# Seven matmuls that nobody reads, a last product taken bank by bank, and a new order for 3800 units

## The chip, the cores and the metric

The kernel runs on one core of one Trainium2 chip. The metric is device time in microseconds of one execution, inputs and outputs in device memory. Before the change the median of three runs is 907.4 us (907.23 to 908.23). Engines are named TensorE (PE in the rows; PEld is its loading of weights), VectorE (DVE), ScalarE (ACT), GpSimd (POOL) and SyncE (SP, which here only issues transfers).

## The reference

Attention over pooled keys and values, and a gated feed-forward layer on its result. All is float32.

```python
# q, k, v: (8, 8, 576, 64); w_gate, w_val: (512, 1536); w_out: (1536, 512)
k_p = k.reshape(B, H, 72, 8, D).mean(axis=3)
v_p = v.reshape(B, H, 72, 8, D).mean(axis=3)
scores = scale * np.matmul(q, k_p.transpose(0, 1, 3, 2))
scores = scores - np.max(scores, axis=-1, keepdims=True)
attn = np.exp(scores)
attn = attn / (np.sum(attn, axis=-1, keepdims=True) + 1e-09)
attn_out = np.matmul(attn, v_p)
x = np.ascontiguousarray(attn_out.transpose(0, 2, 1, 3)).reshape(4608, 512)
gate = 1.0 / (1.0 + np.exp(-(x @ w_gate)))
out = (gate * (x @ w_val) @ w_out).astype(np.float32)
```

## The kernel before

The 4608 tokens are cut into nine blocks of 512. The first block is done alone: its attention, its two products with the gate and value weights, and its product with the output weights. The other eight go in four pairs, where a scheme of seven block products in place of eight is used. Products of the feed-forward layer run on operands that are split into a high and a low part, three passes for each (`chain` is a bank of the first layer, `acc` one of the second).

The heads are taken two at a time, so a block has four pairs of heads. For each pair of the first block: VectorE adds up the keys in groups of eight (`keys`, the rows `early<-h`, later `early<-raw`), ScalarE places the sums on a block diagonal (`kbd`), TensorE makes the scores in two halves (`sc`), VectorE takes the maximum and subtracts it, ScalarE takes the exponential, VectorE sums and multiplies by the reciprocal (`main`, whose result is a 512-column tile), TensorE turns it (`tp`), ScalarE copies the turned tile out, and TensorE multiplies by the values (`av`). The 8 keys of 72 that don't fit into 64 rows go apart, as `rest`, `r` and `tr`. GpSimd clears the `kbd` tiles, places keys of later blocks, makes some low parts of the weights, and issues some transfers. A score instruction in float32 appears as two passes in the rows.

The order of all this is neither that of the code nor a scheduler's. Every instruction is taken down in a book, a few of them together as one unit (`Book.unit`), and the units are then issued in the order of a long table of numbers, `LATER`, one list for all engines; each engine runs its instructions in that order. So a unit waits behind those ahead of it in the list on its own engine, and for its operands. All instructions are issued from the helper `call` (line 317), so that all rows have that line.

The part that the change touches in the code is the last product (`second_sums`, line 1069, with `result`, line 1073) and the beginning of `first_pass` (line 1147). In `second_sums` each unit `(m, q)` multiplies a piece of the hidden layer with a piece of the weights, for two row blocks `k` and two banks `c`. The last results go out in half rows: ScalarE copies 256 columns out of the bank, SyncE sends them, and so on, four times.

Of the kernel before, what the change touches and what calls it, by code (L numbers as in the profile page):

```python
# [19 lines left out]
P = 128  # L20
# [9 lines left out]
BT = 512  # L30
# [82 lines left out]
5 4 3 6 0 10 2 7 24 13 17 19 20 8 26 12 27 18 16 30 9 22 21 75 25 34 36 35 46 32 1 44 39 54 38 40 11 29 47 28 51 15 31  # L113
65 52 66 37 61 57 41 67 62 42 14 60 63 53 73 82 45 74 70 87 79 71 97 136 84 123 77 112 109 111 80 88 100 99 101 96 98
59 83 104 91 105 89 81 106 72 130 78 107 110 93 92 95 94 58 114 127 115 116 119 125 86 103 120 128 197 144 122 143 142
135 141 85 137 138 129 157 205 140 147 145 121 102 204 134 132 153 154 152 133 155 151 131 222 90 108 139 118 161 203
164 149 124 162 148 216 126 163 156 167 150 166 189 170 158 169 174 159 165 146 171 190 160 55 168 177 179 243 172 173
117 178 56 193 180 186 230 181 223 182 199 244 233 201 196 206 200 202 209 185 184 33 188 225 192 49 191 176 195 240
175 236 183 187 234 226 247 239 238 250 245 251 259 217 248 257 282 253 242 258 212 279 283 64 276 252 232 261 286 267
237 43 269 211 278 50 256 274 219 268 254 218 277 266 265 231 275 272 241 280 221 299 288 298 284 228 305 227 229 285  # L120
289 292 113 302 290 281 293 255 235 273 294 303 316 300 246 326 332 329 304 333 335 301 311 287 318 331 330 328 327
317 334 307 308 306 198 309 314 352 322 260 312 315 325 362 324 353 208 364 291 345 323 366 339 313 346 348 338 365
349 321 340 296 399 350 360 310 215 376 68 342 405 361 341 297 358 343 214 344 69 367 347 295 263 382 355 373 370 337
264 374 380 224 375 270 271 377 336 371 386 387 356 385 354 395 357 372 398 396 397 393 411 392 403 402 48 207 368 391
400 412 363 417 406 410 407 369 419 378 404 409 401 388 418 416 389 408 414 413 424 426 320 447 319 425 23 423 381 427
422 262 379 446 429 420 384 434 421 383 194 444 430 220 457 437 435 431 578 466 436 483 441 485 443 452 449 451 492
210 428 469 470 467 468 464 461 493 462 213 463 450 432 433 497 486 500 390 440 487 415 501 448 438 456 584 471 484
472 480 498 481 477 490 439 458 473 517 482 502 249 478 479 460 521 513 465 474 491 475 499 530 454 453 531 590 488
532 527 476 510 522 489 524 528 394 525 445 523 685 529 504 526 507 495 540 546 496 516 545 505 459 519 506 514 494
455 511 534 442 544 533 542 512 503 577 541 551 548 520 582 535 556 518 549 557 558 76 596 567 560 568 570 571 536 569  # L130
611 564 543 603 574 572 550 580 606 581 351 565 515 555 566 561 554 612 562 539 573 604 576 607 632 563 605 597 600
579 598 552 583 608 538 601 537 602 599 648 622 623 559 642 629 553 627 669 359 678 636 575 628 672 953 659 656 675
588 591 679 613 585 633 586 676 667 660 593 595 594 589 680 666 587 592 673 614 677 609 670 610 621 508 674 615 630
618 624 626 697 634 700 509 689 616 631 635 617 619 637 690 620 643 625 639 649 682 684 671 694 701 653 652 640 686
645 646 687 650 651 698 699 655 702 657 691 703 692 662 638 647 641 695 654 696 681 711 708 658 668 663 644 714 693
661 726 704 715 665 547 706 727 664 707 709 710 712 683 717 718 729 720 722 713 719 725 724 705 721 730 731 728 737
735 723 952 743 760 733 761 747 745 954 736 746 739 738 752 748 740 755 762 744 768 732 765 763 955 751 758 759 775
756 757 764 767 782 766 805 750 753 771 993 806 754 772 1101 787 777 770 774 783 769 789 784 795 800 776 788 797 716
779 801 780 807 785 793 741 792 773 799 804 819 825 822 796 794 816 956 831 786 778 802 815 823 781 840 828 824 817
829 833 803 850 851 826 810 830 867 852 820 827 853 809 854 871 864 837 855 821 847 848 808 856 818 742 857 841 878  # L140
849 879 881 882 749 863 883 858 734 902 921 688 875 903 862 836 884 811 925 904 813 814 880 917 791 812 885 861 838
832 876 872 859 994 844 957 888 835 1056 843 996 845 889 842 865 886 920 866 868 891 899 958 890 905 870 992 860 1102
900 877 961 869 893 873 834 892 874 901 839 1103 1104 959 906 960 894 962 922 1106 895 915 995 978 908 923 972 1105
932 1048 979 1046 924 981 918 846 896 897 1047 887 973 909 941 898 907 933 911 938 942 982 1110 934 980 935 926 929
983 912 913 936 1111 1107 949 1112 790 1049 997 1108 919 1113 939 1109 998 1166 999 943 1050 1002 1051 910 1000 1001
937 969 1057 927 1134 1022 916 1063 940 944 914 1023 1093 950 946 963 945 964 1058 1027 947 951 965 1167 984 966 1024
# [1423 lines left out]
```

## Time and profile before

| | |
|---|---|
| median of 3 runs | 907.4 us |
| the profiled execution | 906.58 us |
| its span, first to last instruction | 904.8 us |
| TensorE busy | 891.4 us |
| VectorE busy | 657.4 us |
| ScalarE busy | 544.5 us |
| GpSimd busy | 200.0 us |

The profile is of one execution. The span is shorter than the time of the execution, which has a start and an end outside of the engines' instructions. A row of the view in order of time has the start, the length, the engine, the operation with its written and read tiles, a count where equal instructions follow each other, and in brackets how long the engine was idle before it and what ended that. Matmuls overlap: a pass is listed as 0.39 us although the next one starts 0.23 us after it, so that costs of passes are taken from the length of a run of them, not from one.

### The profile page before, as it was taken

How to read it: one execution, taken by the hardware profiler on the slowest of the kernel's cores; microseconds unless marked ns; L12 is line 12 of the kernel's file. 1: busy time of each engine (PE TensorE's matmuls, PEld its weight loads, DVE VectorE, ACT ScalarE, POOL GpSimd, SP SyncE). 2: the span in 40 equal slices, each digit the busy share in tenths (PEclk: the TensorE clock that was granted, in tenths of full speed). 3: DMA queues.
4: the chain of work that ended last, by engine and by line, in shares of the span. 5: the costliest groups of instructions: out<-in, count | busy, mean ns of one | idle time of the engine just before them, and what ended most of it. 6: DMA issues, size and time to landing. Idle time of an engine off the chain costs nothing.

```text
span 904.8 us, 12625 instructions
## 1 busy us (share of the span) xinstructions
PE 891.4 (99%) x4148; PEld 732.7 (81%) x4148; DVE 657.4 (73%) x1038; ACT 544.5 (60%) x1110; POOL 200.0 (22%) x369
## 2 busy tenths in 40 slices
PE   6999999999999999999999999999999999999998
PEld 5788878888888888888888888888888888888886
DVE  7989888889899999756668796355589552224863
ACT  5998998788978476545375555445365552224352
POOL 2422101012164235443443104132213000000000
PEclk9999999999999999999999999999999999999999
DMA  9899888889999888787987877676747776645554
GB/s 337 309 326 336 301 335 298 298 285 338 320 324 316 276 287 286 237 299 259 308 276 237 244 273 264 229 268 194 264 122 252 245 249 207 228 167 204 192 169 143
DMA packets 100433, 237.56 MB, mean 263 GB/s; under 512 B 13872, under 2 KB 34992, under 8 KB 98832
## 3 DMA queue, kind: packets, MB, share of 16 engines
q1 hardware_dynamic: 85328, 203.97, 66.6%
q0 software_dynamic: 15040, 32.79, 10.4%
q8 instruction: 33, 0.54, 0.2%
q14 instruction: 32, 0.26, 0.1%
HBM read 176.02 MB, written 60.69 MB: 262 GB/s over the span
## 4 chain that ended last, share of the span: by engine, by line
PE 81%; ACT 2%; DVE 1%; issue 0%; ACTq 0%
PE chain L317 50%; PE acc L317 25%; PE av L317 3%; PE sc L317 3%; ACT hs L317 0%; DVE s L317 0%; DVE hs L317 0%; PE tp L317 0%; DVE h L317 0%; ACT e L317 0%; ACT L317 0%; ACT raw_o L317 0%; DVE w_o L317 0%; ACT w_o L317 0%; ACT oparts L317 0%
## 5 line engine op out<-in xcount | busy, mean ns | idle before, releaser
L317 PE MATMUL chain<-xo,parts 128*128 128x512 f32 x2316 | 544.1, 392 | 0.5 <-ACT xs L317 0.5
L317 PEld LDWEIGHTS chain<-xo,parts 128*128 128x128 f32 x2316 | 430.7, 188 | 93.3 <-issue 1.0
L317 PE MATMUL acc<-hs,oparts 128*128 128x512 f32 x1008 | 237.0, 391 | 0.2 <-issue 0.2
L317 PEld LDWEIGHTS acc<-hs,oparts 128*128 128x128 f32 x1008 | 188.1, 188 | 40.6 <-DVE hs L317 1.2
L317 POOL DMA_DIRECT2D turned<-turn x240 | 131.7, 551 | 214.3 <-DVE turn L317 184.3
L317 DVE TENSOR_TENSOR y<-chain,sV 128x512 f32<-128x512 f32 x46 | 31.1, 686 | 69.6 <-PE chain L317 54.7
L317 ACT CAST hs<-h 128x1024 fp32r<-128x1024 f32 x52 | 54.3, 1051 | 27.2 <-PE acc L317 22.4
L317 DVE TENSOR_TENSOR hs<-h,hs 128x1024 fp32r<-128x1024 f32 x52 | 63.0, 1217 | 10.5 <-ACT hs L317 10.3
L317 ACT COPY chain<-chain 128x512 f32<-128x512 f32 x46 | 26.5, 577 | 52.8 <-PE chain L317 45.8
L317 DVE TENSOR_TENSOR y<-chain,sG 128x512 f32<-128x512 f32 x46 | 31.2, 682 | 34.2 <-PE chain L317 23.4
L317 ACT CAST hs<-s 128x1024 fp32r<-128x1024 f32 x36 | 37.5, 1050 | 28.5 <-DVE s L317 13.0
L317 DVE TENSOR_TENSOR hs<-s,hs 128x1024 fp32r<-128x1024 f32 x36 | 43.8, 1218 | 11.1 <-ACT hs L317 10.9
L317 ACT COPY sG<-chain 128x512 f32<-128x512 f32 x46 | 26.6, 584 | 41.0 <-PE chain L317 39.4
L317 ACT ACT_TABLE_LOAD x37 | 47.5, 1283 | 0.6
L317 ACT COPY sV<-chain 128x512 f32<-128x512 f32 x46 | 26.7, 584 | 34.0 <-PE chain L317 32.7
L317 ACT ACTIVATE gate<-chain 128x512 f32<-128x512 f32 x46 | 26.9, 594 | 31.8 <-PE chain L317 29.4
L317 DVE TENSOR_TENSOR h<-chain,gate 128x512 f32<-128x512 f32 x46 | 30.7, 679 | 20.1 <-PE chain L317 20.0
L317 PE MATMUL sc<-kbd,raw 128*128 128x144 f32 (+1 forms) x262 | 41.4, 297 | 0.3 <-ACT pr L317 0.2
L317 PEld LDWEIGHTS sc<-kbd,raw 128*128 128x128 f32 (+1 forms) x262 | 33.5, 176 | 8.6 <-issue 2.8
L317 ACT ACTIVATE gate<-y 128x512 f32<-128x512 f32 x46 | 28.9, 632 | 17.0 <-DVE y L317 16.8
L317 PE MATMUL acc<-oparts,hs 128*128 128x512 f32 x144 | 38.7, 402 | 0.0
L317 DVE TENSOR_REDUCE m<-sc 128x4 f32<-128x288 f32 x48 | 21.7, 452 | 17.5 <-PE sc L317 17.2
(210 smaller groups left out, 1099.9 us busy)
## 6 DMA issues: line engine op xcount, KB each, us to landing
oparts<-keptS SPq DMA_DIRECT2D x48, 512.0 KB, 4.7
oparts<-keptO SPq DMA_DIRECT2D x72, 256.0 KB, 4.7
raw<-in_wgv SPq DMA_DIRECT2D x12, 1024.0 KB, 8.1
out<-o SPq DMA_DIRECT2D x34, 256.0 KB, 3.8
raw<-in_kT SPq DMA_DIRECT2D x28, 288.0 KB, 5.0
raw<-in_qT SPq DMA_DIRECT2D x29, 256.0 KB, 4.9
raw<-in_vm SPq DMA_DIRECT2D x24, 256.0 KB, 5.5
raw_o<-in_wo SPq DMA_DIRECT2D x12, 512.0 KB, 8.5
```

The costliest lines, as they stand in the source:

```text
L317: return self._book.take(lambda: f(*args, **named))
```

## The change

Three edits. Ahead of the first scores, seven matmuls are issued that multiply the last cleared `kbd` tile with itself and write a bank of which nothing is read. In the last unit of the last product the two banks are taken one after the other, bank 0 with both row blocks and then bank 1, where before each row block went over both banks. And the last results go out otherwise: bank 0 whole, by ScalarE and one transfer of SyncE; bank 1 in halves, one copied by ScalarE and sent from ScalarE's queue, one copied by VectorE and sent by SyncE. Besides, the table `LATER` is another one throughout.

```diff
 LATER = """
-5 4 3 6 0 10 2 7 24 13 17 19 20 8 26 12 27 18 16 30 9 22 21 75 25 34 36 35 46 32 1 44 39 54 38 40 11 29 47 28 51 15 31
...
-            if last and side and add is None:
-                for k in (0, BT // 2):
-                    nc.scalar.copy(t[:, k:k + BT // 2], bank[:, k:k + BT // 2])
-                    nc.sync.dma_start(outT[r:r + P, a + k:a + k + BT // 2], t[:, k:k + BT // 2])
+            if last and side and add is None and c:
+                x, y = slice(0, BT // 2), slice(BT // 2, BT)
+                nc.scalar.copy(t[:, x], bank[:, x])
+                nc.vector.tensor_copy(t[:, y], bank[:, y])
+                nc.scalar.dma_start(outT[r:r + P, a:a + BT // 2], t[:, x])
+                nc.sync.dma_start(outT[r:r + P, a + BT // 2:a + BT], t[:, y])
                 return
...
-            for k in range(2):
+            final = last and i + 1 == len(units)
+            for n1 in range(2):
                 with book.unit():
-                    for c in range(2):
+                    for k, c in ((0, n1), (1, n1)) if final else ((n1, 0), (n1, 1)):
...
-                if i == 0 and k == 1:
+                if i == 0 and n1 == 1:
...
+        idle = ps.tile([P, HT, 2 * KEYS], F32, name="idle", tag="tp")
+        with book.unit():
+            for _ in range(7):
+                nc.tensor.matmul(idle[:, 0], lhsT=kbd[RING - 1][:, :P], rhs=kbd[RING - 1], start=True, stop=True)
+
```

What the new table does at three places follows, as the instructions stand on an engine; a line with - is of before, one with + of the changed kernel. First TensorE at the program's start (`kbd_89` to `kbd_92` are the four pairs' keys of the first block, `kbd_93` is the fifth tile of the ring):

```order
+L317 MATMUL idle<-kbd_93 128x144 x7
 L317 MATMUL sc<-kbd_89,h 128x144 x4
 L317 MATMUL sc<-kbd_90,h 128x144 x4
 L317 MATMUL sc<-kbd_91,h 128x144 x4
+L317 MATMUL sc<-kbd_92,early 128x144 x2
 L317 MATMUL vr<-xs_220 96x2x64 x4
-L317 MATMUL sc<-kbd_92,early 128x144 x4
+L317 MATMUL sc<-kbd_92,early 128x144 x2
```

The seven stand ahead of all scores, and one half of the fourth pair's scores goes ahead of a product with values. On SyncE, at the same place, keys (`in_kT`) and queries (`in_qT`) of the first block and the block of constants (`in_const`) are sent for:

```order
+L317 DMA h<-in_kT 128x576
+L317 DMA h<-in_qT 128x512
 L317 DMA h<-in_kT 128x576 x2
 L317 DMA h<-in_qT 128x512
 L317 DMA h<-in_kT 128x576
+L317 DMA early<-in_qT 128x512
 L317 DMA cst<-in_const 128x133
 L317 DMA h<-in_qT 128x512
-L317 DMA h<-in_kT 128x576
-L317 DMA h<-in_qT 128x512
-L317 DMA early<-in_qT 128x512
```

The first query is now second and not third, the constants eighth and not fifth, one query ninth. The second place is VectorE where the first block's third and fourth pair of heads get their probabilities. Before (the `128x512` rows are these two products, the reductions of `raw` are keys of the second block, `vres` low parts of values):

```order
L317 TENSOR_REDUCE early<-early 128x8 x2
L317 TENSOR_SCALAR early<-early 128x16
L317 TENSOR_TENSOR vres_104<-vr,vres_104 32x128
L317 RECIPROCAL early<-early 128x16
L317 TENSOR_TENSOR rest<-early 128x128
L317 TENSOR_TENSOR early<-early 128x512
L317 CAST r_261<-rest 128x4x32
L317 TENSOR_REDUCE early<-raw 128x72
L317 TENSOR_TENSOR early<-early 128x512
```

And in the changed kernel:

```order
L317 TENSOR_REDUCE early<-early 128x8 x2
L317 TENSOR_REDUCE early<-raw 128x72
L317 TENSOR_SCALAR early<-early 128x16
L317 RECIPROCAL early<-early 128x16
L317 TENSOR_TENSOR vres_105<-vr,vres_105 32x128
L317 TENSOR_TENSOR rest<-early 128x128
L317 TENSOR_TENSOR early<-early 128x512
L317 CAST r_262<-rest 128x4x32
L317 TENSOR_TENSOR early<-early 128x512
```

The reduction of the next block's keys has moved from behind the first of the two products to ahead of both. The third place is ScalarE at the program's end, with what each instruction waits for in brackets. Before:

```order
L317 CAST hs<-h 128x1024 [waits DVE_49,PE_49] x2
L317 COPY o<-acc 128x256 [waits DVE_49,PE_49]
L317 COPY o<-acc 128x256
L317 COPY o<-acc 128x256 [waits PE_49]
L317 COPY o<-acc 128x256
```

And in the changed kernel:

```order
L317 CAST hs<-h 128x1024 [waits PE_49,Activation_49]
L317 CAST hs<-h 128x1024 [waits DVE_49,PE_49] x2
L317 COPY o<-acc 128x512 [waits DVE_49,PE_49]
L317 COPY o<-acc 128x256 [waits DVE_49]
L317 DMA out<-o 128x256 [waits DMAHW3_49,Activation_49]
```

Four copies became two, and the second waits for VectorE, whose copy of the other half of that bank is its last instruction.

## Rows read from the trace of the kernel before

**Rows 1.** The page, busy time of each engine, and VectorE and TensorE in 40 slices of the span.

```profile
PE 891.4 (99%) x4148; PEld 732.7 (81%) x4148; DVE 657.4 (73%) x1038; ACT 544.5 (60%) x1110; POOL 200.0 (22%) x369
...
PE   6999999999999999999999999999999999999998
...
DVE  7989888889899999756668796355589552224863
```

**Rows 2.** The page, the chain of work that ended last, by engine.

```profile
PE 81%; ACT 2%; DVE 1%; issue 0%; ACTq 0%
```

**Rows 3.** The table by stretches: from and to, length, then busy time of each engine with its instructions, the granted clock of TensorE, the share of DMA time, GB/s.

```profile
0.00:5.51 5.51, 0.00 (x0) 0.03 (x1) 1.48 (x2) 2.24 (x5) 2.63 (x21) 1.00 0.65 198
5.51:9.84 4.33, 4.33 (x16) 3.85 (x16) 3.19 (x8) 1.00 (x5) 0.00 (x0) 1.00 1.07 377
9.84:12.40 2.56, 2.20 (x16) 1.93 (x16) 2.56 (x7) 1.60 (x4) 0.00 (x0) 1.00 0.98 330
12.40:20.66 8.26, 6.61 (x38) 5.16 (x37) 8.13 (x24) 6.36 (x16) 1.03 (x1) 1.00 1.04 390
20.66:27.52 6.86, 6.86 (x35) 4.38 (x35) 6.61 (x12) 5.33 (x10) 3.90 (x5) 1.00 0.99 404
27.52:900.73 873.21, 871.39 (x4047) 717.39 (x4045) 635.48 (x989) 527.34 (x1072) 192.40 (x343) 1.00 0.77 260
900.73:904.80 4.07, 0.00 (x0) 0.00 (x0) 0.00 (x0) 0.65 (x3) 0.00 (x0) 0.93 0.38 131
```

**Rows 4.** The view in order of time, TensorE in the head.

```profile
5.51 4.33 PE L317 MATMUL sc<-kbd,h 128*128 128x144 f32 x16 [5.51 <-DMA h<-in_qT]
10.02 1.22 PE L317 MATMUL sc<-kbd,h 128*128 128x144 f32 x8 [0.18 <-issue]
...
14.95 0.55 PE L317 MATMUL tp<-cst,early 128*128 128x128 f32 x3 [0.91 <-DVE early L317]
...
20.66 0.63 PE L317 MATMUL tp<-cst,early 128*128 128x128 f32 x4 [0.56 <-DVE r L317]
...
27.52 12.55 PE L317 MATMUL chain<-xo,parts 128*128 128x512 f32 x54
```

**Rows 5.** The same view, VectorE in the head.

```profile
3.72 1.48 DVE L317 TENSOR_REDUCE early<-h 128x72 f32<-128x576 f32 x2 [3.72 <-DMA h<-in_kT]
...
6.66 0.75 DVE L317 TENSOR_REDUCE early<-h 128x72 f32<-128x576 f32 x1 [1.46 <-DMA h<-in_kT]
...
19.83 0.68 DVE L317 TENSOR_TENSOR early<-early 128x512 f32<-128x512 f32 x1
20.43 0.22 DVE L317 CAST r<-rest 128x128 fp32r<-128x128 f32 x1
20.56 0.74 DVE L317 TENSOR_REDUCE early<-raw 128x72 f32<-128x576 f32 x1
21.23 0.68 DVE L317 TENSOR_TENSOR early<-early 128x512 f32<-128x512 f32 x1
```

**Rows 6.** The same view, GpSimd's clearing of the `kbd` tiles and ScalarE's placing of the first keys.

```profile
0.78 0.83 POOL L318 MEMSET kbd<- 128x144 f32 x5
...
4.57 0.53 ACT L317 ACTIVATE kbd<-early 64x72 f32<-64x72 f32 x2 [2.33 <-DVE early L317]
```

**Rows 7.** The same view, SyncE's issue of the last query, and two groups of the view of transfers (KB of each, median us from issue to landing).

```profile
4.50 0.43 SPq L317 DMA_DIRECT2D early<-in_qT  x1
...
early<-in_qT SPq DMA_DIRECT2D x1, 256.0 KB, 5.2
...
cst<-in_const SPq DMA_DIRECT2D x1, 66.5 KB, 4.2
```

**Rows 8.** The view of waits, TensorE from 27 us on: all that is listed (in total, times, longest).

```profile
PE tp L317 <- ACT y L317: 0.5, 1, 0.5
PE chain L317 <- ACT xs L317: 0.5, 1, 0.5
PE tr L317 <- ACT early L317: 0.2, 1, 0.2
PE sc L317 <- ACT pr L317: 0.2, 1, 0.2
PE acc L317 <- issue: 0.2, 1, 0.2
```

**Rows 9.** The chain that ended last in order of time (start, length, what, passes), two long runs of passes.

```profile
733.37 108.45 PE chain L317 x474
...
844.54 47.60 PE acc L317 x210
```

**Rows 10.** The end of the program: the view in order of time, the instructions on the tile `o` (duration in ns as least, median and most), and the last transfers' group.

```profile
900.09 1.33 ACT L317 COPY o<-acc 128x256 f32<-128x256 f32 x4 [6.86 <-PE acc L317]
900.48 1.79 SPq L317 DMA_DIRECT2D out<-o  x4
...
L317 SPq DMA_DIRECT2D out<-o x10: 332/341/426, 880.1 to 901.9; - x10
L317 ACT COPY o<-acc x6: 372/379/589, 879.5 to 901.0; 128x256 f32<-128x256 f32 x4, 128x512 f32<-128x512 f32 x2
L317 DVE TENSOR_TENSOR o<-acc,sG x2: 684/688/691, 883.5 to 891.5; 128x512 f32<-128x512 f32 x2
...
out<-o SPq DMA_DIRECT2D x4, 128.0 KB, 1.8
```

## What was predicted before the result

> **What bounds the kernel now.** I read the page's busy shares first [rows 1]: TensorE is busy 99% of the span, VectorE 73%, and the chain of work that ended last is 81% TensorE [rows 2]. Then the table by stretches [rows 3], which says where the missing per cent lies. From 27.52 to 900.73 us TensorE is busy 871.39 of 873.21 us: only 1.82 us of visible idle in the long middle. Everything else lost is at the ends: 5.51 us before the first matmul, 0.36 us until 12.40, 1.65 us from 12.40 to 20.66, and 4.07 us behind the last matmul. So the change can gain in three places: head, middle, tail.
>
> In the head the view of instructions in order of time [rows 4] shows two things. The first 16 score passes take 4.33 us, the next 8 only 1.22. Per pass that is 0.27 against 0.15 us, though the table gives a granted clock of 1.00 in every stretch [rows 3]; I read the first as the 1.2 GHz level and the second as 2.4 GHz. But VectorE [rows 5] waits until 6.66 us for its third block of keys, and from there it hardly stops: 2.56 of 2.56 us and 8.13 of 8.26 us busy in the two stretches up to 20.66 [rows 3]. TensorE's last long wait, 0.56 us, ends at 20.66 with VectorE's release (it stands in the row as VectorE's "r"), just behind the product that makes the third pair's probabilities (19.83 plus 0.68); from 20.66 to 27.52, where the first chain matmul stands, TensorE is busy throughout [rows 3, 4, 5]. VectorE paces the head; the scores do not.
>
> The trace's execution took 906.58 us for a span of 904.8, so 1.78 us lie around it; the median of the runs is 907.4, 0.8 above the profiled one. I sum changes of the span and add them to the median.
>
> **Unread matmuls.** Seven instructions, two passes each by the count of the scores (4 instructions make 8 passes), so 14 passes. At the slow price of 0.27 they take 3.8 us. Their operand is the last of the five blocks that GpSimd clears by 1.61 [rows 6], so they run from about 1.65 to 5.4. Queued behind them stand all scores. The first could start at about 5.15, because the first query is now the second transfer and the first keys are placed on ScalarE by 5.10 [rows 6]; the delay of up to 0.3 us falls into VectorE's wait for keys. If they raise the clock, 16 passes shrink from 4.33 to 16 times 0.15, 2.4 us: 1.9 us off TensorE. Bounds: 1.9 gained if scores were on the path, nothing if VectorE covers them. I take nothing: VectorE has no wait for a score in it after 6.66. If that cover went, the gain would be back up to 1.9.
>
> **Order of the head.** The keys that VectorE reduces third are still the fourth transfer; what is gone ahead of its landing is the constant block, 66.5 KB beside four blocks of 256 to 288 KB that need until 6.66 [rows 5, 7], some 0.2 us at their rate. So VectorE begins its unbroken run about 0.2 us earlier. Against that the key reduction of the next block, which stood behind the product of the third probabilities, now stands ahead of it (the order, in the part on the change): 0.67 us from its start to the next one's [rows 5]. It was hidden; now it is on the path, since the first transposition of that product and, queued behind it, the first attention product wait for it. From there to the first chain matmul the same 8 transpositions, 4 small ones, 4 attention products and 5 scores follow as before, 6.86 us of TensorE work [rows 3]. Sum: +0.67 less 0.2, taken as +0.4. Bounds: -0.3 (the waits between dependent small VectorE operations are filled by the reduction) to +1.0. Late next would be ScalarE's copies of the transposed probabilities, 0.59 each; they are made beside the attention products.
>
> **Order of the middle.** 3800 units are laid out anew. The work is the same; only waits can change. At most the 1.82 us of visible idle can go, of which the two longest single waits, both for ScalarE, are 0.5 each [rows 8]. Besides, there are pauses too short to count as idle: 474 chain passes took 108.45 us, 0.2288 each, 210 accumulating ones 47.60, 0.2267 [rows 9]; 2.1 ns over 474 passes is 1 us in 108, and as much everywhere would be 8 us. No row shows TensorE waiting for GpSimd long enough to be listed [rows 8], so room for late results of GpSimd removes nothing that this trace shows. Nor does the trace show the new order; bounds are -3.8 (all visible idle and a quarter of the short pauses) and +1.8 (as much idle again). I take -0.4, a quarter of the visible idle, nearest to losing one of the two 0.5 us waits.
>
> **The tail.** Before, the last twelve passes alternate between two banks; ScalarE makes four half copies from 900.09 in 1.33 us, and SyncE issues four transfers from 900.48 to 902.27, each landing 1.8 us later [rows 10]. So the last issue, at about 901.9, sets the end. Now bank 0 is ready three passes earlier, 0.68 us, and one transfer carries it. Bank 1 is ready as before, when the third half copy began, 900.76. Its halves are copied by VectorE, then ScalarE: the order gives ScalarE's copy a wait for VectorE. Two copies of about 0.4 (the ScalarE ones took 0.38 each; VectorE's nearest row is 0.69 for 512 columns; both [rows 10]) end at 901.6, and ScalarE issues its own transfer then. That is 0.3 before 901.9. Bounds: -0.6 (the first half's transfer is what counts) to +0.4 (a first transfer on ScalarE's queue is slower; no row has one). I take -0.3. Nothing is queued behind these waits. The rule that speaks against more: the Trainium skill's "PSUM — Partial Sum Buffer", in "PSUM bank collisions raise a hardware error", says that two engines must not touch one bank's quadrant at once, two reads included. By it the halves cannot be copied side by side, which would have made the gain 0.7; the wait in the order is in line with it, and no run here shows the collision.
>
> **Sum.** 0 + 0.4 - 0.4 - 0.3 = -0.3; 907.4 - 0.3 = 907.1 us. Less than 0.2%, 1.8 us, is about what a measurement of this kernel cannot tell from no change (its three runs lie 1.0 apart).
>
> **Rivals.** (a) The new order takes the middle's pauses away: all 1.82 of visible idle and two of the 8 us of short pauses, with the tail -4.1, with the head -3.7: 903.7 at the far end, 905.0 at two thirds of it. For it: pauses are spread all over [rows 9]. Against: the work stays, and no single wait is longer than 0.5 [rows 8], so many places have to improve at once. Chance 0.22. (b) The middle gets new waits: plan and chip part somewhere, and as much idle is added as was there, 1.8, plus the head's upper bound, 1.0, less the tail: 907.4 + 2.5 = 909.9. For it: every wait of TensorE that the trace lists there is for a result 0.2 to 0.5 us late [rows 8], so producers already stand close ahead of their readers. Chance 0.12. (c) The clock falls back, the slower side. With faster scores, TensorE is through the first two pairs by about 8 us (9.84 less 1.9 [rows 4]) and has nothing until the third pair's query is there; that is now the ninth transfer, and the old ninth, issued at 4.50, landed 5.2 later, at 9.7 [rows 7]. That is a wait of 1.7 us or more behind the raised clock, where the longest one in the head before was 0.91 [rows 4]. If it falls there, the 6.61 us of passes between 12.40 and 20.66 run at the slow level for half or all of that stretch: +3.3 to +6.6, of which the stretch's 1.65 us of idle absorbs half at best; about +3 is left: 910.1. It decides once passes behind that wait show 0.27 again. Against: 0.91 us did not lower it. Chance 0.06. The Trainium skill's "TensorE: Matmul & The Clock Gate", in "HAM oscillation — how this bites in real kernels", says that waits between bursts put the array back to half rate; the trace shows no fall behind its own short waits, so it doesn't test that. (d) The unread matmuls pay in full, because a faster score lets VectorE do more before its keys come: -1.9 with the rest as summed, 905.2. Against: VectorE's three first key reductions stand ahead of any score in the new order. Chance 0.05.
>
> **Chances and range.** The forecast, no measurable change, 0.55. Faster by over 0.2%: (a) and (d), 0.27. Slower: (b) and (c), 0.18. The likeliest case alone lies between 905.8 and 908.7. The range takes in two thirds of (a) and (d) below and most of (b) above: 904.9 to 909.3.
>
> **What would show it.** In the new profile: scores from about 5.3 us at 0.15 per pass in their greater part (the clock), VectorE without idle from about 6.5 to 20 all the same (no gain from it); the third pair's transpositions at about 21.0 and the first chain matmul at 27.7 to 28.1 (the head's +0.4); visible idle of TensorE of 1 to 2 us from there to its last pass; last transfer issued at about 1.3 us behind the last pass's start, from ScalarE. The forecast is wrong if the first chain matmul stands before 27.0, or if visible idle in the middle is above 3 us, or if passes turn slow again after 8 us.

## The result and the profile after

The changed kernel takes 914.1 us, median of three runs (913.06 to 914.25); the ratio to the kernel before is 1.0063, 95% interval 1.0048 to 1.0079. It is slower, and outside the predicted range. A second series of the same kernel, run beside the experiments, gave 912.05 (six runs, 910.49 to 913.77), ratio 1.0043 (1.0026 to 1.0059). The profiled execution took 914.1 us for a span of 912.3.

The page: busy share of TensorE, the granted clock in 40 slices, and the chain that ended last by engine.

```profile
PE 898.4 (98%) x4162; PEld 738.0 (81%) x4162; DVE 656.2 (72%) x1039; ACT 544.0 (60%) x1108; POOL 203.4 (22%) x369
...
PEclk8999999999999999999999999999999999999999
...
PE 79%; ACT 9%; DVE 5%; DMA 5%; issue 2%; SPq 0%; DVEq 0%; ACTq 0%
```

The busy shares are those of [rows 1] within a percentage point. The shares of the chain can't be set beside [rows 2]: the chain of before is followed back only to 131.43 us of its span, this one to the start. In two traces of the old order whose chain reaches the start (`unread_again` and `tail_only`, both below) ScalarE, VectorE and transfers have 10% and 12% of it, here 19%. The table by stretches, cut where the granted clock changes (from and to, length, busy time of TensorE, weight loads, VectorE, ScalarE and GpSimd, clock, share of DMA time, GB/s), answers to [rows 3]:

```profile
5.50:12.22 6.72, 3.19 (x22) 2.79 (x23) 5.75 (x13) 2.19 (x7) 0.00 (x0) 1.00 1.03 348
12.22:19.05 6.83, 6.83 (x27) 5.91 (x26) 5.33 (x16) 3.16 (x8) 1.33 (x1) 0.50 1.02 402
19.05:30.23 11.18, 10.72 (x58) 7.39 (x56) 10.96 (x23) 9.66 (x20) 4.72 (x6) 1.00 0.75 296
30.23:193.13 162.90, 159.45 (x776) 129.12 (x774) 140.47 (x240) 143.44 (x343) 28.52 (x39) 1.00 0.87 311
193.13:196.54 3.41, 3.41 (x11) 2.76 (x9) 2.07 (x5) 0.67 (x2) 0.00 (x0) 0.50 0.62 194
196.54:908.00 711.46, 710.65 (x3264) 586.66 (x3264) 490.46 (x746) 382.55 (x726) 166.21 (x303) 1.00 0.75 248
908.00:912.30 4.30, 0.39 (x2) 0.00 (x0) 0.42 (x1) 0.37 (x1) 0.00 (x0) 1.00 0.33 122
```

Twice the granted clock is 0.50, the 1.2 GHz level: for 6.83 us in the head and for 3.41 us from 193.13 on. Before, the only stretch below 1.00 lay behind the last matmul (0.93 in [rows 3]). The time before the clock's first rise counts as 1.00 in these tables, although its passes take 0.27 us, so a figure below 1.00 tells of falls alone. Cut at the first chain matmul and at the start of the last pass, the account of the two profiled executions is:

| | before | after | difference |
|---|---|---|---|
| start to the first chain matmul | 27.52 | 30.23 | +2.71 |
| from there to the last pass's start (the middle) | 872.82 | 877.77 | +4.95 |
| from there to the end | 4.46 | 4.29 | -0.17 |
| span | 904.8 | 912.3 | +7.5 |

TensorE's waits in the middle, the two longest in the view (total, times, longest), against [rows 8]:

```profile
PE tp L317 <- DVE pm L317: 1.8, 1, 1.8
PE chain L317 <- ACT parts L317: 0.5, 1, 0.5
```

The first of them stands directly ahead of the fall of the clock at 193.13. In the head TensorE's rows, in order of time, answer to [rows 4]:

```profile
1.66 3.73 PE L317 MATMUL idle<-kbd 128*128 128x144 f32 x14 [1.66 <-POOL kbd L318]
5.50 1.22 PE L317 MATMUL sc<-kbd,h 128*128 128x144 f32 x8
7.98 1.22 PE L317 MATMUL sc<-kbd,h 128*128 128x144 f32 x8 [1.26 <-DMA h<-in_qT]
11.47 1.59 PE L317 MATMUL sc<-kbd,h 128*128 128x144 f32 x8 [2.27 <-ACT kbd L317]
12.86 1.30 PE L317 MATMUL sc<-kbd,early 128*128 128x144 f32 x4
```

The unread passes take 0.27 us each, the first scores behind them 0.15: the clock has risen before the first score. Then TensorE waits 1.26 us for the second pair's query and 2.27 us for ScalarE's placing of the third pair's keys, and four passes that take 0.73 us without a fall (`no_unread`, below) take 1.30. The second trace of the changed kernel waited only 0.43 us for the query, but again 2.27 us for the keys, and its clock was at half for 10.24 us:

```profile
11.58 2.29 PE L317 MATMUL sc<-kbd,h 128*128 128x144 f32 x8 [2.27 <-ACT kbd L317]
```

```profile
10.83:21.07 10.24, 9.49 (x34) 8.39 (x35) 8.26 (x23) 5.60 (x11) 1.50 (x1) 0.50 1.01 388
```

### The profile page after: what moved, and what is told of

The parts are those of the page before. It is cut to its first block, busy times and chain, and to the rows that moved or that the text cites. A ratio compares the mean times of both kernels' runs of the same rounds, so it can differ in the third digit from the quotient of the medians.

```text
span 912.3 us, 12659 instructions
## 1 busy us (share of the span) xinstructions
PE 898.4 (98%) x4162; PEld 738.0 (81%) x4162; DVE 656.2 (72%) x1039; ACT 544.0 (60%) x1108; POOL 203.4 (22%) x369
## 4 chain that ended last, share of the span: by engine, by line
PE 79%; ACT 9%; DVE 5%; DMA 5%; issue 2%; SPq 0%; DVEq 0%; ACTq 0%
PE chain L317 43%; PE acc L317 28%; PE sc L317 3%; PE av L317 3%; DMA raw<-in_qT 1%; ACT parts L317 1%; ACT e L317 1%; ACT L317 1%; DMA raw<-in_kT 1%; DMA raw<-in_wgv 1%; ACT raw L317 1%; DMA w<-keptWO 1%; DVE early L317 1%; DVE h L317 1%; ACT w L317 1%
```

## The experiments

The first chain matmul and the middle of every trace that is used below, with the median time (and its lowest and highest). The kernel before, run beside each series, had medians of 907.05 to 907.42 us:

| kernel | first chain | middle | time |
|---|---|---|---|
| before | 27.52 | 872.82 | 907.4 |
| after | 30.23 | 877.77 | 914.1 (913.06 to 914.25) |
| after, again | 31.53 | 876.17 | 912.05 (910.49 to 913.77) |
| no_unread | 28.18 | 875.00 | 912.47 (909.31 to 914.97) |
| unread_only | 27.80 | 872.94 | 906.45 (905.49 to 907.98) |
| unread_again | 27.55 | 872.80 | 906.85 (905.78 to 908.96) |
| bridge | 28.25 | 875.27 | 911.05 (908.53 to 914.33) |
| head_new | 28.79 | 872.53 | 908.85 (907.75 to 910.53) |
| mid_new | 27.16 | 875.43 | 909.9 (908.55 to 912.09) |
| key_after_pm | 30.53 | 874.39 | 910.79 (909.22 to 917.16) |
| key_no_unread | 30.13 | 874.81 | 910.89 (909.13 to 912.42) |
| early_new | 27.56 | 880.19 | 909.7 (908.35 to 914.35) |
| late_new | 27.83 | 874.28 | 909.06 (906.25 to 913.37) |
| late_turn | 27.99 | 874.56 | 908.89 (907.58 to 911.08) |
| mended_again | 28.37 | 874.50 | 909.1 (908.29 to 910.32) |
| tail_only | 27.90 | 873.12 | 907.33 (906.84 to 908.62) |

A trace is one execution, and the new order scatters: a row's trace need not lie at its median. In the eight traces with the old order in the head the first chain matmul comes between 27.16 and 27.99 us; in the five traces with the old order in the middle that takes 872.53 to 873.12.

**The unread matmuls, out of the new order and into the old one.** `no_unread`:

```diff
         with book.unit():
-            for _ in range(7):
-                nc.tensor.matmul(idle[:, 0], lhsT=kbd[RING - 1][:, :P], rhs=kbd[RING - 1], start=True, stop=True)
+            pass
```

> The changed kernel without its seven unread matmuls (the unit stays in the order, empty; order and tail as changed). Theory of the clock: the unread matmuls bring full speed at 5.4 us, the scores then run ahead of their data, TensorE waits 1.26 and 2.27 us, and the granted clock falls to half from 12.22 to 19.05 us; without them full speed comes only near 10 us and stays, the first chain matmul starts at 27.6 to 28.2 us instead of 30.23, and the time is 914.1 less 2.0 to 2.6, 911.5 to 912.1. Rival, that the new head order (key reduction ahead of the product) makes the loss: the first chain matmul stays at 29.5 us or later and the time at 913.5 to 914.3. Both expect the pause of 1.8 us near 191 us to stay.

The first chain matmul came at 28.18, as the theory of the clock has it, and the mean granted clock was 0.999 or 1.000 in all six executions (0.994 to 0.996 in the first three of the changed kernel). But the trace is of the fastest of the six, 909.31, and the median, 912.47, lies where neither put it, with a scatter of 5.7 us and no fall of the clock. It is no lower than the 912.05 of the changed kernel's second series. The pause at 191 us, which both expected to stay, wasn't in this trace. So the head was told right for this trace and the middle not understood: the kernel loses without any fall of the clock, and differently from execution to execution.

`unread_only` puts the same seven matmuls ahead of the old order:

```diff
+        idle = ps.tile([P, HT, 2 * KEYS], F32, name="idle", tag="tp")
+        with book.unit():
+            for _ in range(7):
+                nc.tensor.matmul(idle[:, 0], lhsT=kbd[RING - 1][:, :P], rhs=kbd[RING - 1], start=True, stop=True)
```

> The kernel before with nothing but the seven unread matmuls ahead of its first scores (old order, old tail). Theory of the clock: full speed from 5.4 us, a wait of 2 us or more for the third pair's operands, the granted clock back at half near 12 us; first chain matmul at 29.5 to 30.3 us instead of 27.52, time 909.4 to 910.2. Rival, that the order makes the loss: the first chain matmul within 0.3 us of 27.5 and 907.2 to 907.7. Middle and tail as before in both.

No loss: 906.45, ratio 0.9991 (0.9982 to 1.0001), and no fall of the clock in ten executions (0.999 or 1.000). The theory's expectation fell: unread matmuls alone don't bring the clock down. In this trace the clock rose only at 10.86, so it left open what an early rise does. Run again:

> The kernel before with the seven unread matmuls alone, a second time, since 906.45 against 907.26 was at the edge of what can be told. Theory that they help a little where the old order keeps the third pair's scores close behind the second's: 906.3 to 906.9 and no fall of the granted clock even where it rises before 7 us; rival, that it was chance: 907.2 to 907.6. Third, that an early rise of the clock is followed by a fall here too: single runs at 909 or above with a mean clock of 0.998 or less.

906.85, ratio 0.9994 (0.9984 to 1.0005): a gain is not told apart from chance. In this trace the clock rose at 6.32 and stayed. TensorE's first rows:

```profile
1.67 3.73 PE L312 MATMUL idle<-kbd 128*128 128x144 f32 x14 [1.67 <-POOL kbd L313]
5.58 1.57 PE L312 MATMUL sc<-kbd,h 128*128 128x144 f32 x8 [0.18 <-DMA h<-in_qT]
7.61 1.22 PE L312 MATMUL sc<-kbd,h 128*128 128x144 f32 x8 [0.45 <-DMA h<-in_qT]
10.00 1.25 PE L312 MATMUL sc<-kbd,h 128*128 128x144 f32 x8 [1.18 <-ACT kbd L312]
```

The waits are 0.45 and 1.18 us where the new order has 1.26 and 2.27: there ScalarE ends the third pair's placing at 11.42, behind an exponential, here at 9.94. One of twelve executions had a mean clock of 0.996, at 908.96, the highest, which all but meets the third of the sentences expected. A mean clock of 0.998 or less is what one slow stretch of 3.41 us makes of it. Counted over the executions of all runs with a change in the order or with unread matmuls, it was found thus:

| head | unread matmuls | executions with a fall |
|---|---|---|
| new order | seven | 25 of 29 |
| new order | none | 1 of 16 |
| new order | seven, and eleven in the waits (`bridge`, next, and the two kernels built on it) | 4 of 31 |
| old order | seven | 1 of 22 |
| old order, the new one behind it (`mid_new`, `early_new`, `late_new`, `late_turn`, below) | none | 3 of 42 |

So the fall comes as a rule where both meet, the unread matmuls and the new order's late third pair, and now and then with one of them or none. The mean doesn't tell where in an execution a fall lies.

**Work through the waits.** `bridge` leaves the new order as it is and adds unread matmuls ahead of the second and the third pair's scores:

```diff
+BRIDGE = {(0, 1, 1): 4, (0, 2, 0): 7}
...
         with book.unit():
+            for _ in range(unread):
+                nc.tensor.matmul(sc[:, 0], lhsT=kbd[RING - 1][:, :P], rhs=kbd[RING - 1], start=True, stop=True)
             for i in range(HT):
```

> The changed kernel with eleven more unread matmuls: four ahead of the second pair's scores and seven ahead of the third pair's, so that TensorE works through the waits of 1.26 and 2.27 us. Theory of the clock: where it has risen before 7 us it doesn't fall back, the first chain matmul starts at 28.0 to 28.5 us instead of 30.2 and the time falls by about 2. Where it rises only at 9 to 11 us, as in another kernel with unread matmuls, the eleven run at half speed, 0.27 a pass for 22 passes, and the third pair comes up to 2 us late. Rival, that the fall at 12 us doesn't hang on the waits: it comes as before, first chain matmul at 30 us or later, and the time is 914 or more.

```profile
5.31 1.22 PE L318 MATMUL sc<-kbd,h 128*128 128x144 f32 x8
6.37 1.14 PE L318 MATMUL sc<-kbd 128*128 128x144 f32 x8
7.63 1.22 PE L318 MATMUL sc<-kbd,h 128*128 128x144 f32 x8
8.68 1.88 PE L318 MATMUL sc<-kbd 128*128 128x144 f32 x14
10.98 1.25 PE L318 MATMUL sc<-kbd,h 128*128 128x144 f32 x8 [0.42 <-ACT kbd L318]
12.34 0.76 PE L318 MATMUL sc<-kbd,early 128*128 128x144 f32 x4
```

The rows `sc<-kbd` without `h` are the added ones. With TensorE at work the clock stays (granted clock 1.00 from 4.88 until behind the last matmul), and the first chain matmul comes at 28.25 instead of 30.23. Seven of the ten executions had a mean clock of 0.999 or 1.000; three, at 911.24, 912.53 and 914.33, had 0.998, and where their fall lay isn't known. The theory of the clock holds for the head: the fall hangs on the waits, and the first chain matmul is 2.0 us later with it. In the time of the whole kernel this can't be told from chance: against the 912.05 of the same series the median fell by 1.0, half of the 2 expected, within the scatter.

**Head and middle by themselves.** The tables were put together from both orders (`new` and `old`, in the numbers of the changed code):

```diff
-LATER = new
+LATER = new[:161] + [u for u in old if u not in new[:161]]
```

> The changed kernel with the old order behind the first chain matmul: the head stands in the new order with its unread matmuls, the 3,600 units behind it in the order of before, the tail as changed. Theory that the two losses add, each from its own stretch: first chain matmul near 30.2 us where the clock falls back (28.2 where it doesn't), the middle 872.8 to 873.3 us as before, time 907.3 + 2.7 = 910.0 where the clock falls, 908.0 where not. Rival, that a late head is made up later: 907.2 to 907.8.

908.85, 1.4 us over its kernel before, ratio 1.0010 (1.0000 to 1.0020): what the new head costs by itself, its order and its clock together. The middle is 872.53, no worse than before, and the clock was at half for 3.41 us in the head, from 11.45; eight of the ten executions had a fall. The theory's condition "where the clock falls" has degrees: with the new head the slow stretch was 3.41, 6.83 and 10.24 us in different traces, and the first chain matmul came at 28.79, 30.23 (30.53 in another) and 31.53. `mid_new` is the complement, without unread matmuls:

```diff
-LATER = new
+LATER = old[:156] + [u for u in new if u not in old[:156]]
```

> The changed kernel with the old order ahead of the first chain matmul and without the unread matmuls: old head, new order behind it, tail as changed. Theory that the new order loses by itself in the middle: first chain matmul at 27.5 to 28.0 us, the middle 875.0 to 877.8 us instead of 872.8 (both seen with this order), time 909.5 to 912.3, and more scatter than the kernel before, which lies within 1.5 us of its median. Rival, that the middle's pauses follow from the late head: 907.2 to 907.8.

909.9, ratio 1.0024 (1.0011 to 1.0037), middle 875.43, no fall in any of the ten executions: as the theory said. The new order loses 2.5 us in the middle by itself, with the old head and a full clock. The 1.4 of `head_new` and these 2.5 make 3.9 of the 4.6 that the second series of the changed kernel lost. That second series:

> The changed kernel as it is, a second time, beside the others of this call. Both theories expect 913 to 914.5; the pause at 191 us and the clock's fall behind it are expected again if the key's transfer is late in every execution, and are gone if that was chance (the kernel without unread matmuls showed no such pause in its one trace): then the middle is 874.5 to 875.5 us instead of 877.8.

The time, 912.05, is below the 913 that both expected at least. The pause at 191 us was 0.5 us this time, with no fall of the clock behind it, and another of 2.16 us stood at 464 us, where the first trace had none. So neither sentence on the pause was right: pauses come and go at several places.

**One pause, repaired.** In the changed kernel's first trace the rows around 191 us are (SyncE's issue, VectorE, TensorE):

```profile
181.06 0.83 SPq L317 DMA_DIRECT2D raw<-in_kT  x1
...
190.64 0.75 DVE L317 TENSOR_REDUCE ks<-raw 128x72 f32<-128x576 f32 x1 [2.01 <-DMA raw<-in_kT]
191.31 0.68 DVE L317 TENSOR_TENSOR h<-h 128x512 f32<-128x512 f32 x1
191.91 0.69 DVE L317 TENSOR_TENSOR pm<-e,rz 128x512 f32<-128x512 f32 x1
...
190.14 0.80 PE L317 MATMUL sc<-kbd,raw 128*128 128x144 f32 x6
192.74 0.73 PE L317 MATMUL tp<-cst,pm 128*128 128x128 f32 x4 [1.79 <-DVE pm L317]
```

VectorE stands still for a key block's transfer, 9.6 us after its issue; the product `pm` that TensorE needs next is two places behind. SyncE issued that transfer behind four others from 178.61 on. In the old order it stood behind one store and a query and landed after 3.6 us; in all seven traces with the old order there it took 3.4 to 5.1, in eight other traces with the new order there 6.7 to 10.2. That the place in SyncE's queue is the reason is likely and not shown by itself. `key_after_pm` moves one unit, number 1184:

```diff
-1184 1065 1046 1022 1264 1015 1260 1053
+1065 1046 1022 1264 1015 1260 1053 1184
```

> The changed kernel with one VectorE unit moved: the key reduction that waits 2.0 us for its transfer at 188.6 us is issued behind the product pm instead of two places ahead of it. Theory: that reduction is what holds pm back, so TensorE's pause of 1.8 us at 190.9 us goes, and with it the fall of the granted clock from 193.13 to 196.54 us: 1.96 us of pause and 1.75 us of slow passes less, 914.1 - 3.7 = 910.4 (910.0 to 911.0). Rival, that the reduction is needed as early as it comes (the copy to kbd and the scores behind it wait instead): the pause moves to a score some 2 us later and the time stays within 1 us of 914.1.

```profile
188.50 0.69 DVE L312 TENSOR_TENSOR h<-h 128x512 f32<-128x512 f32 x1 [0.70 <-DMA h<-keptwG]
189.11 0.68 DVE L312 TENSOR_TENSOR pm<-e,rz 128x512 f32<-128x512 f32 x1
190.45 0.75 DVE L312 TENSOR_REDUCE ks<-raw 128x72 f32<-128x576 f32 x1 [0.66 <-DMA raw<-in_kT]
...
190.07 0.66 PE L312 MATMUL tp<-cst,pm 128*128 128x128 f32 x4
```

The transfer is as late as before (10.2 us), VectorE still waits for it, and TensorE doesn't: no pause, no fall of the clock behind it (the head has its fall as before), the middle 874.39, 3.4 less than in the changed kernel's first trace, and the median 910.79 as expected. Beside the second series, whose trace had only 0.5 us of this pause, it is 1.3 less. The edit does what it was to do at its place; how often the pause came without it isn't known. With this edit and without the unread matmuls:

> The changed kernel without its unread matmuls and with the key reduction behind pm, both at once. Theory that the two causes are separate and add: against the 912.05 of the changed kernel beside the same runs, some 2 us for the head (first chain matmul at 28.2 instead of 30.2 to 31.5) and some 1.3 for the reduction (912.05 to 910.79), 908.8; range 908.3 to 910. Rival, that without the clock's fall the key's transfer is in time anyway, so that the second edit gives nothing more: as without unread matmuls alone, 911 to 912.5.

910.89: 2 us above what adding would give. In this trace the clock rose only at 15.88 and the first chain matmul came at 30.13; without unread matmuls the head can be late too. (Its first 24 score passes take 2.26 us for eight, the price at 1.2 GHz; in the seven other traces without unread matmuls the clock rose between 8.84 and 11.27.) The middle was 874.81. The rival's figure is the one that was met, but not for its reason; the run doesn't decide between them. Beside the 910.79 with the unread matmuls, taking them out gave nothing, as in `no_unread`.

**Where in the middle.** `early_new` takes the new order up to about 231 us and the old one behind it, `late_new` the reverse, both with the old head and no unread matmuls (`mid` is the table of `mid_new`):

```diff
-LATER = mid
+LATER = mid[:1298] + [u for u in old if u not in mid[:1298]]
```

```diff
-LATER = new
+LATER = old[:1298] + [u for u in new if u not in old[:1298]]
```

> Old head without unread matmuls, then the new order for the units up to about 231 us, then the old order; tail as changed. With the new order all the way behind the old head the time was 909.9 (907.4 before). Theory that the new order loses where transfers are dense, up to some 230 us (by 50 us from the first chain matmul its pauses stood 0.5, 1.2, 0.1 and 0.4 us above those of before, and 0.4 us above in all that follows): 909.5, 909.0 to 910.0. Rival, that the loss is spread evenly: a quarter of it, 908.0.

> The complement: the order of before up to about 231 us, the new order from there on; tail as changed, no unread matmuls. Theory that the loss lies ahead of 231 us: 907.4 + 0.4 = 907.8, 907.3 to 908.3. Rival, evenly spread: three quarters of the 2.5 us, 909.3.

909.7 (ratio 1.0032, 1.0019 to 1.0046) and 909.06 (1.0015, 0.9997 to 1.0032). The first is the theory's figure, the second is not: the two halves lose 2.65 and 2.0 against their kernel before, and the whole 2.5. Each half seems to suffice, though the interval of `late_new` just takes in no loss (its trace's middle, 874.28, is 1.2 us above the highest with the old order); the seam between two orders may have a price of its own, which these runs don't separate. But the trace of `early_new` is its slowest execution, 914.35, and shows the mechanism at a third place:

```profile
110.47 1.13 ACT L312 ACTIVATE w<-raw 128x1024 f32<-128x1024 f32 x1 [2.45 <-DMA raw<-in_wgv]
111.51 1.21 ACT L312 ACTIVATE raw<-raw,cst 128x1024 uint32<-128x1024 uint16 x1
112.62 0.57 ACT L312 CAST pr<-tr 96x512 fp32r<-96x512 f32 x1
...
113.24 0.76 PE L312 MATMUL sc<-kbd,raw 128*128 128x144 f32 x4 [1.74 <-ACT pr L312]
```

ScalarE waits 2.45 us for a weight block, the copy `pr` stands behind it, TensorE waits 1.74 us, and from 115.52 to 118.93, behind a further wait of 0.49 us, the granted clock is 0.50. The same instruction waited 0.93 us in the changed kernel's first trace (TensorE then 0.24) and not at all in that of `no_unread`. `late_turn` moves one unit in `late_new`, the transposition `turn` behind the product `y`. Its row names no releaser, but the last store out of such a tile from GpSimd's queue lands 0.27 us before it starts in the trace of `late_new`, and 0.28 us before in the second trace of the changed kernel:

```diff
-2311 2517 2514
+2517 2514 2311
```

> Old order up to 231 us and the new order behind it (909.06 with a scatter from 906.25 to 913.37), with one unit moved: turn behind y. Theory that the pause at 459 us (1.6 us in its trace) is what scatters this kernel: no pause above 0.9 us near 459 us, median 907.2 to 908.0, scatter 2 us or less above the lowest. Rival: the median stays within 0.5 us of 909 and the scatter as wide.

The pause near 459 us is gone and the highest run is 911.08 instead of 913.37, but the median is 908.89: on the median the rival holds. That the pause made the long runs is not shown either: the profiled run of `late_new` had it, with 1.44 us of waiting on TensorE, and took 908.73, less than its median. The pause that the edit removes reads thus in the second trace of the changed kernel:

```profile
464.82 0.71 DVE L317 STREAM_TRANSPOSE turn<-pm 128x512 f32<-128x512 f32 x1 [2.44 <-issue]
465.45 0.65 DVE L317 TENSOR_TENSOR y<-chain,sV 128x512 f32<-128x512 f32 x1
...
466.16 1.20 PE L317 MATMUL chain<-xo,parts 128*128 128x512 f32 x4 [2.16 <-DVE y L317]
```

**All repairs at once.** `mended` is `bridge` with both moved units, no other edit (the changed lines of the table):

```diff
-1184 1065 1046 1022 1264 1015 1260 1053
+1065 1046 1022 1264 1015 1260 1053 1184
...
-2311 2517 2514
+2517 2514 2311
```

> The changed kernel with three repairs, each for one pause that its traces showed: eleven more unread matmuls through the waits of the head, the key reduction behind pm (191 us), and the transpose turn, which waits for stores from GpSimd's queue, behind the product y that TensorE's next chain run needs (463 us, 2.3 us in one trace, 1.5 in two others). Theory that the loss is the clock's fall in the head and a few VectorE instructions that wait for transfers ahead of urgent work: first chain matmul at 28.2 us, the middle 874.0 to 875.0, no pause above 0.9 us, time 908.7 (908.0 to 909.3), with less scatter than the 908.5 to 914.3 of the kernel with the head's repair alone. Rival, that the scatter has many more places than these: the median stays at 910 or more and new pauses of 1 to 2 us stand at other places.

Ratio 1.0013 (1.0000 to 1.0027), median 909.06 of eleven executions (907.47 to 910.64); the twelfth, the profiled one, took 3,187 us, and no line of its trace is used. So the kernel ran again for a trace:

> The kernel with the three repairs once more, for its trace. Theory: full clock from its rise to the end, first chain matmul near 28.2 us, no pause above 0.9 us at 191 or 463 us, the middle 874.0 to 875.0 us, some 1.5 to 2 us above the 872.8 of before in pauses below 0.9 us; time 908.7 to 909.4. Rival: pauses of 1 to 2 us at other places, middle above 875.5 us.

909.1, ratio 1.0021 (1.0011 to 1.0030), lowest and highest 2.0 us apart where `bridge` had 5.8. The two moved places, VectorE at 460 us and TensorE at 189 us, and the middle's stretch:

```profile
460.43 0.69 DVE L313 TENSOR_TENSOR y<-chain,sV 128x512 f32<-128x512 f32 x1 [0.35 <-PE chain L313]
461.04 0.70 DVE L313 STREAM_TRANSPOSE turn<-pm 128x512 f32<-128x512 f32 x1
...
188.84 0.66 PE L313 MATMUL tp<-cst,pm 128*128 128x128 f32 x4
```

```profile
5.50:28.37 22.87, 21.17 (x125) 16.96 (x125) 21.95 (x50) 14.88 (x33) 6.09 (x7) 1.00 0.97 364
28.37:902.87 874.50, 872.25 (x4046) 717.26 (x4045) 633.09 (x988) 526.96 (x1070) 195.24 (x342) 1.00 0.77 260
```

Every figure of the theory was met: clock 1.00, first chain matmul 28.37, middle 874.50, and no pause above 0.5 us in the middle (the longest in the head is 1.02 us, at 21.44, for VectorE's `r`). The changed kernel lost 4.6 us beside its kernel before (912.05 against 907.42), the repaired one 1.95 (909.1 against 907.15). So the repairs together took away 2.7 us; the medians don't share them out. What is left, 0.85 us in the head and 1.68 in the middle of this trace, isn't traced to single units here. Of the 1.68 only 0.43 is visible idle (2.25 us, where before had 1.82); the other 1.25 stands in pauses too short to count as idle, which lengthen TensorE's busy time. The cause of this rest stays open.

**The tail alone**, in the old order (the tail's part of the change with its six units, nothing else):

```diff
-            if last and side and add is None:
+            if last and side and add is None and c:
...
-            for k in range(2):
+            final = last and i + 1 == len(units)
+            for n1 in range(2):
```

> The kernel before with nothing but the last product taken bank by bank and the last copies and stores of the change. From the traces: last pass to the end of the span 4.30 us against 4.46, so 907.4 - 0.16 = 907.2; the prediction's own term was -0.3, 907.1. Rival, that what the tail gives depends on the new order: no change or a loss, 907.4 to 907.8.

907.33 against 907.26, ratio 1.0001 (0.9991 to 1.0010): nothing. From the last pass's start to the end it is 4.67 us in this trace, 4.46 before, 4.29 after.

Neither the change nor its repair beats the kernel before; the best that ran is the old order with the unread matmuls, and that isn't told apart from it.

## Why the prediction was wrong

**What bounds the kernel** was read rightly for the old order, though not from the 81% of [rows 2], which are of a chain followed back only to 131.43 us, and with one slip (the clock is 0.93, not 1.00, in the last stretch of [rows 3]) on which nothing hangs: with the clock up from 6.32 us its first chain matmul came at 27.55, so VectorE, not the scores, sets the head. It was not carried over to the new order, where the fall of the clock put TensorE itself on the path (busy 6.83 of 6.83 us in the slow stretch, VectorE 5.33).

**Unread matmuls, 0.** Right in the old order (906.45 and 906.85, neither told apart from no change), wrong in the new one, by the traces: the first chain matmul came 2.0 us later (30.23 against 28.25 with the waits filled). In the order of time this is the first step that failed. The medians don't bear out a loss of that size: 912.47 without the unread matmuls against 912.05 with them, 910.89 against 910.79, and 1.0 us gained by `bridge`; the new head as a whole lost 1.4 (`head_new`). Its mechanism stood among the rivals, as (c), at 0.06, with its price (+3 against +2.0) and its sign: the clock falls behind a wait of 1.7 us or more. The wait that counted was not the one for a query, as (c) had it (1.26 us, and 0.43 in the second trace), but the one for the third pair's keys on ScalarE (2.21 to 2.30 us in all four traces with a fall in the head). The objection that weighed it down, that 0.91 us had not lowered the clock, compared a short wait with a long one: 1.18 us in `unread_again` and 1.59 in `no_unread` did not lower it either. The Trainium skill's "TensorE: Matmul & The Clock Gate", in "HAM oscillation — how this bites in real kernels", says that waits between bursts of matmuls put the array back to half rate; this trace agrees in kind, with 1.22 us of scores between 1.26 and 2.27 us of waiting and the clock at 0.50 after them, though its waits are shorter than those of the page's example.

**Order of the head, +0.4.** Where the clock stayed the first chain matmul came at 28.18, 28.25 and 28.37: +0.66 to +0.85 against 27.52, inside the bounds of -0.3 to +1.0. The sign was right and the size somewhat too small, as far as three traces tell beside an old head that scatters from 27.16 to 27.99.

**Order of the middle, -0.4.** The term that failed by most, and enough alone: `mid_new`, with the old head and without unread matmuls, lost 2.5 us (909.9, ratio 1.0024). It was +4.95 in the profiled execution, outside its bounds of -3.8 to +1.8, and +1.6 to +2.6 in the traces of the whole new middle without a long pause. The step asked how much of TensorE's visible idle could go or come, by [rows 8], and took the longest waits there, 0.5 us, as the measure of a new one. But in the long pauses what became late was not a product at the edge of its time: an in-order engine stood in front of a transfer (VectorE at 191 and at 464 us, ScalarE at 110 us in `early_new`). How near such an engine stands to its transfers is read from VectorE's and ScalarE's waits for them, and from what each load stands behind on SyncE, which the step did not look at. The smaller loss, 1.68 us, that remains where no long pause is left has no cause shown; the short pauses, which the step counted only as something to gain, grew by 1.25 us there. Rival (b), new waits in the middle, was the right case, at 0.12, with +2.5 in all.

**Rivals as alternatives.** (b) and (c) came true together, and their sum was never formed: 1.8 for the middle, 3 for the clock, 0.4 to 1.0 for the head's order, less 0.3 for the tail, make 4.9 to 5.5, between the measured 4.6 and 6.7 (that it fits so well is in part luck, since the medians show less than 3 for the clock). Both can hang on the same thing, a new order with closer transfers, so that one makes the other likelier; that is an argument, not a result.

**The tail, -0.3.** Nothing that can be told. The order of events was as worked out: last issue from ScalarE, 1.35 us behind the last pass's start at 908.00 (1.3 said), its copy waiting for VectorE's:

```profile
908.95 0.37 ACT L317 COPY o<-acc 128x256 f32<-128x256 f32 x1 [1.30 <-DVE o L317]
909.35 0.37 ACTq L317 DMA_DIRECT2D out<-o  x1
```

Against the 1.56 of before (901.9 less 900.34) that is 0.2 earlier, within what the tails of different traces scatter (4.29 to 4.85 with the new tail).

Of the signs named beforehand two came: passes turning slow after 8 us, and visible idle in the middle above 3 us (877.77 less the stretches' busy time gives 4.3).

## What to carry to other kernels

An order can be worth less than its matmuls show: before a reordering is taken, look at every instruction on an in-order engine that waits for a transfer, at what it holds up, and at how many transfers the load now stands behind. Put such an instruction behind the urgent ones, and the transfer's lateness need not reach TensorE, as the trace of `key_after_pm` shows with a transfer of 10.2 us. And work that warms TensorE needs real work behind it without long waits; otherwise it moves the slow stretch from passes that nobody waits for to passes on the path. Even where the clock stayed up no run here shows that it paid.

## What had not been expected of the hardware

With the same seven unread matmuls from 1.67 us on, the clock rose at 4.6, 4.9, 5.4, 6.2, 6.3, 7.4, 7.6 and 10.9 us in eight traces: the program alone doesn't set it (5.4 and 7.4 are two traces of the changed kernel itself). The slow stretch behind it, where there was one, was 3.41, 6.83 or 10.24 us long. One pause of 1.8 us in otherwise full work (TensorE busy 159.45 of 162.90 us up to then) was followed by a fall of 3.41 us that cost seven passes 0.20 to 0.34 us each, some 1.5 in all; one of 1.74 us, with another of 0.49 close behind, was followed by the same in `early_new`, while one of 2.16 us at 464 us was followed by none. And one and the same transfer landed 9.6 and 8.2 us after its issue in two traces of the same program, and 6.7 to 10.2 in nine traces with the new order there.
